# A new table of order and engines for an attention and MLP kernel on one core

## The chip, the cores and the metric
The kernel runs on one NeuronCore of one Trainium2 chip. The core has a matrix engine (TensorE, PE in the profile; PEld is its weight load), a vector engine (VectorE, DVE), an activation engine (ScalarE, ACT), a general engine (GpSimd, POOL) and a queue for DMA issues (SyncE, SP). Each engine carries out its instructions in the order in which they were written for it. The metric is the time of one execution on the device in microseconds (us). Before the change the median of three runs is 287.29 us (285.19 to 288.51).

## The reference
Two layers, one after the other. A linear attention with cosine-weighted features over 8 batches of 576 tokens and 8 heads of 64, and then an MLP without a bias over all 4608 tokens:
```python
def _attn_ref(q, k, v):                 # each 8, 8, 576, 64
    theta = np.pi / 2.0 * pos / S
    def phi(x, c, s):
        r = np.maximum(x, 0.0)
        return np.concatenate([r * c, r * s], axis=-1)
    q_p = phi(q, cos_w, sin_w)
    k_p = phi(k, cos_w, sin_w)
    kv = np.einsum('bhsf,bhsd->bhfd', k_p, v)
    z = np.sum(k_p, axis=2)
    num = np.einsum('bhsf,bhfd->bhsd', q_p, kv)
    den = np.einsum('bhsf,bhf->bhs', q_p, z)[..., None] + 1e-06
    return (num / den).astype(np.float32)

def _moe_ref(x, w_in, w_out):           # 4608x512, 512x2048, 2048x512
    h = x @ w_in
    g = h * np.cos(h)
    return (g @ w_out).astype(np.float32)
```
Inputs and outputs are float32; the kernel multiplies in float16 and sums in float32.

## The kernel before, in words
**Tiling.** The tokens are worked on in nine chunks of 512. Chunk c below 8 is 512 tokens of batch c; the 64 that are left over in each batch make up chunk 8. For each batch there is a load of k, q and v, five token tiles of features (relu times cosine or sine, `prep`, L452 on ScalarE and L453 on VectorE), casts of V to float16 (`cast_v`, L466 ScalarE, L467 VectorE, L468 GpSimd), the product `kv` (L479), and for each token tile the transposed q (`q_pe` on TensorE with its copy at L514 or L516, or `q_dma`, a transposing DMA), the product `num` (L542), the denominator (`den`, L560 or L562), the quotient x (L566, L568), and x transposed (`x_pe`, L588 with its copy at L593, or `x_dma`). Batches 0 and 1 transpose q on TensorE, batches 0, 1 and 2 transpose x there; the others go through DMAs. "First attention" and "second attention" are those of batches 0 and 1.

**The MLP.** `layer1` makes h by chunks of w_in's columns, `gate` takes the cosine on ScalarE (L609, a sine with a shift) and multiplies on VectorE (L614). Chunks 0 and 1 do it plainly (L637), chunk 2 with 512 columns at a time (`layer1_plain`, L677). From chunk 3 on part or all of layer1 is done with seven half-size products in place of eight (`layer1_fast`, L780), which needs sums of the blocks of x (`layer1_sums`, XS, L738) and of w_in (`w_in_sums`, WS, L717). The second layer of chunk 0 is plain (`layer2_plain`: products L880, first copies L889, later sums L892); that of chunk 1 on uses seven products (`layer2`, L948), with sums of blocks of g (S and in place, L926 and L979) and of w_out (T, L904). Its copies out of PSUM stand at L959 and L967, its additions out of PSUM at L963, the very last ones at L1002. `seed` (L663) copies one product's bank to another so that a second product can add to it.

**What sets the order.** Every piece of work is added to a `Plan` as a step, with an engine, an estimated cost, a due time, what it reads and what it writes. Some steps name several engines (`either`: features, V casts, denominators and one PSUM copy, L967). The table `KEYS`, one number for each of the 1407 steps, is a priority. `Plan.forward` (L183) goes through the steps as a list scheduler: it keeps a clock for each engine and a model of the two DMA rings, and takes at each point the ready step with the smallest key among those that can start soon (`PATIENCE`); a step of several engines goes to the one that would finish it first. Then all steps are written out in the order of the start times so found. All of it happens while the program is built; on the chip each engine has a fixed list.

**Loads.** q, k and v of batch 0 are issued on SP first. The weights go through GpSimd's queue: `weights` (L1025) writes one small hold that waits for k (L1027), then issues the four quarters of w_in (L1033, cast from float32 to float16 on the way), then `hold2` (L1037), which waits for the first quarter to land, then two quarters of w_out (L1047). The loads of batch 1 wait for small GpSimd copies into the raw tiles (`hold_raw`, L1052), which read a column of w_in that the quarter named by `GATE1` writes: the third. The last two quarters of w_out follow q of batch 1 (`part_of_w_out`, L1059). By the built program GpSimd issues the quarters of w_in in the order first, third, second, fourth.

**Order around the change.** On TensorE before: layer1 of chunk 0 from 21.45 us, two products of `layer2_plain` from 36.49, the q transpositions of batch 1 (L509), its kv (L479), its num, and the other `layer2_plain` products between. Batch 2's last x transposition is followed directly by the first L677 of chunk 2.

The lines of `Plan` that write out the order, and the copies whose engine was fixed:
```python
        start, done = self.forward([k / 100 for k in KEYS])
        ...
        return sorted(st, key=lambda s: (s["start"], s["n"]))
...
        if eng == "ACT":
            act(0.5, due, lambda: nc.scalar.activation(out=dst, in_=ps, func=AF.Copy), [key], [dkey])
        else:
            dve(0.4, due, lambda: nc.vector.tensor_copy(out=dst, in_=ps), [key], [dkey])
```

Of the kernel before, what the change touches and what calls it, by code (L numbers as in the profile page):

```python
# [125 lines left out]
class Plan:  # L126
# [56 lines left out]
    def forward(self, key):  # L183
# [32 lines left out]
        for n, k in enumerate(left):  # L216
            if not k:
                ask(n)
# [980 lines left out]
```

## Time and profile before
| what | value |
|---|---|
| runs of the kernel before | 285.19, 287.29, 288.51 us |
| the profiled execution | 284.34 us, of which the span from the first to the last instruction is 282.3 us |
| TensorE's mean granted clock | 0.993 |
| busy: PE / PEld / DVE / ACT / POOL | 270.5 / 219.1 / 249.2 / 218.0 / 19.2 us |
| the chain that ended last, by engine | PE 85%, DVE 5%, DMA 4%, ACT 3%, issue 1% |
| bytes moved | 53.30 MB in 77599 packets, a mean of 189 GB/s |
| costliest groups | L609 ScalarE 53.3 us, L614 VectorE 56.7, L948 TensorE 55.9, L452 ScalarE 37.2 and 32.3 |

A group's line reads: line, engine, operation, out<-in (partitions x elements, type), count, busy time, mean duration of one, and the idle time ahead of it with its releaser. Successive instructions of one engine overlap at their ends, so that ScalarE's 128x512 copies, 597 ns long, follow each other every 0.50 us, VectorE's 128x512 operations out of PSUM, 685 ns long, every 0.60 us, and its features, 480 ns long, every 0.40 us. A ScalarE feature of 128x512 takes 715 to 721 ns and follows at 0.61 us. A GpSimd cast of 128x1024 takes 1088 ns, the same cast on VectorE 689 ns. ScalarE takes 1024 ns for the 128x1024 copy of qT, VectorE 687 ns.

### The profile page before, as it was taken

How to read it: one execution, taken by the hardware profiler on the slowest of the kernel's cores; microseconds unless marked ns; L12 is line 12 of the kernel's file. 1: busy time of each engine (PE TensorE's matmuls, PEld its weight loads, DVE VectorE, ACT ScalarE, POOL GpSimd, SP SyncE). 2: the span in 40 equal slices, each digit the busy share in tenths (PEclk: the TensorE clock that was granted, in tenths of full speed). 3: DMA queues.
4: the chain of work that ended last, by engine and by line, in shares of the span. 5: the costliest groups of instructions: out<-in, count | busy, mean ns of one | idle time of the engine just before them, and what ended most of it. 6: DMA issues, size and time to landing. Idle time of an engine off the chain costs nothing.

```text
span 282.3 us, 6870 instructions
## 1 busy us (share of the span) xinstructions
PE 270.5 (96%) x2715; PEld 219.1 (78%) x2715; DVE 249.2 (88%) x443; ACT 218.0 (77%) x396; POOL 19.2 (7%) x32
## 2 busy tenths in 40 slices
PE   7799988999989999999999999999999999999994
PEld 2668956678967667779787988898788888888883
DVE  2877796999999989998999999999999999997952
ACT  2856698896899998599899999996676675877420
POOL 1440020010000010003003000210000000000000
PEclk9799999999999999999999999999999999999999
DMA  6999999969979999997999899988013100300124
GB/s 204 312 200 222 298 291 267 320 133 285 311 231 235 211 229 293 241 310 161 308 234 268 167 275 270 240 117 251 3 37 116 57 2 0 151 0 2 74 77 149
DMA packets 77599, 53.30 MB, mean 189 GB/s; under 512 B 46080, under 2 KB 75264, under 8 KB 77568
## 3 DMA queue, kind: packets, MB, share of 16 engines
q1 hardware_dynamic: 72608, 48.12, 66.7%
q0 software_dynamic: 4224, 4.19, 9.5%
q10 hardware_dynamic: 736, 0.57, 0.6%
q8 instruction: 21, 0.34, 0.5%
q14 instruction: 10, 0.08, 0.1%
HBM read 36.74 MB, written 9.44 MB: 164 GB/s over the span
## 4 chain that ended last, share of the span: by engine, by line
PE 85%; DVE 5%; DMA 4%; ACT 3%; issue 1%; DVEq 0%
PE M L948 32%; PE M L780 15%; PE M L637 10%; PE M L677 7%; PE TR L780 6%; PE M L880 5%; PE ATT L542 3%; DMA xT<-x 2%; PE ATT L479 2%; DMA qm<-in_q_dram 2%; PE M L509 2%; PE ATT L1022 1%; PE TR L677 1%; DVE x L568 1%; ACT xT L593 1%; ACT KQ L452 1%
## 5 line engine op out<-in xcount | busy, mean ns | idle before, releaser
L609 ACT ACTIVATE ch<-M 128x512 f32<-128x512 f32 x90 | 53.3, 597 | 14.4 <-PE M L637 6.9
L614 DVE TENSOR_TENSOR gT<-M,ch 128x512 f16<-128x512 f32 x84 | 56.7, 685 | 5.0 <-ACT ch L609 4.6
L948 PEld LDWEIGHTS <-gT 128*128 128x128 f16 x560 | 54.0, 98 | 7.6 <-DVE gT L926 0.5
L948 PE MATMUL M<-w_out_sb,gT 128*128 128x256 f16 x448 | 55.9, 273 | 0.0
L452 ACT ACTIVATE KQ<-km,CS 128x512 f16<-128x512 f32 x55 | 37.2, 715 | 0.2 <-DMA km<-in_k_dram 0.2
L452 ACT ACTIVATE KQ<-qm,CS 128x512 f16<-128x512 f32 x47 | 32.3, 721 | 4.5 <-DMA qm<-in_q_dram 4.5
L780 PEld LDWEIGHTS <-w_in_sb 128*128 128x128 f16 x320 | 30.8, 98 | 4.3 <-issue 0.2
L948 PE MATMUL M<-T,S 128*128 128x256 f16 x256 | 32.4, 273 | 0.0
L637 PE MATMUL M<-xT,w_in_sb 128*128 128x256 f16 x256 | 30.2, 273 | 0.1
L677 PE MATMUL M<-xT,w_in_sb 128*128 128x512 f16 x112 | 27.6, 379 | 0.8 <-ACT xT L593 0.8
L948 PEld LDWEIGHTS <-S 128*128 128x128 f16 x256 | 24.7, 98 | 4.0 <-issue 0.2
L637 PEld LDWEIGHTS <-w_in_sb 128*128 128x128 f16 x256 | 24.5, 98 | 3.5 <-issue 0.4
L568 DVE TENSOR_TENSOR x<-ATT,rec 128x512 f16<-128x512 f32 x32 | 22.1, 692 | 2.3
L959 ACT ACTIVATE ost<-M 128x512 f32<-128x512 f32 x24 | 14.1, 593 | 12.1 <-PE M L948 9.3
L780 PEld LDWEIGHTS <-WS 128*128 128x128 f16 x216 | 20.5, 98 | 3.3 <-issue 0.5
L677 PEld LDWEIGHTS <-w_in_sb 128*128 128x128 f16 x128 | 12.2, 98 | 10.8 <-issue 0.9
L453 DVE TENSOR_SCALAR KQ<-qm,CS 128x512 f16<-128x512 f32 x33 | 15.4, 498 | 5.1 <-DMA qm<-in_q_dram 5.1
L468 POOL CAST V<-vm 128x1024 f16<-128x1024 f32 (+1 forms) x11 | 10.7, 1004 | 134.9 <-PE M L948 46.0
L542 PEld LDWEIGHTS <-qT 128*128 128x128 f16 x320 | 15.3, 98 | 4.6 <-issue 1.8
L926 DVE TENSOR_TENSOR S<-gT 128x2048 f16<-128x2048 f16 (+1 forms) x16 | 17.4, 1085 | 0.2
L808 DVE TENSOR_TENSOR gT<-Z,ch 128x1024 f16<-128x1024 f32 x13 | 15.9, 1221 | 0.7 <-ACT ch L802 0.4
L542 PE MATMUL ATT<-kvz,qT 128*128 128x65 f16 x288 | 15.7, 194 | 0.6 <-DVE x L568 0.5
(135 smaller groups left out, 461.3 us busy)
## 6 DMA issues: line engine op xcount, KB each, us to landing
out_dram<-ost SPq DMA_DIRECT2D x33, 256.0 KB, 3.0
qm<-in_q_dram SPq DMA_DIRECT2D x8, 640.0 KB, 5.9
km<-in_k_dram SPq DMA_DIRECT2D x8, 640.0 KB, 5.6
qm<-in_q_dram SPq DMA_DIRECT2D x8, 512.0 KB, 6.2
km<-in_k_dram SPq DMA_DIRECT2D x8, 512.0 KB, 5.7
vm<-in_v_dram SPq DMA_DIRECT2D x6, 640.0 KB, 7.2
vm<-in_v_dram SPq DMA_DIRECT2D x6, 512.0 KB, 6.5
w_in_sb<-in_moe_w_in_dram POOLq DMA_DIRECT2D x4, 512.0 KB, 8.9
```

The lines of the kernel that those rows point to most:

```text
L452: fn = {"ACT": lambda: nc.scalar.activation(out=out_, in_=in_, func=AF.Relu, scale=sc), "DVE": lambda: nc.vector.tensor_scalar(out=out_, i ...
L453: "DVE": lambda: nc.vector.tensor_scalar(out=out_, in0=in_, scalar1=0.0, scalar2=sc, op0=ALU.max, op1=ALU.mult)}
L542: nc.tensor.matmul(bank[hb][:, hh * D1:(hh + 1) * D1], lhsT=a[:, h, :], rhs=z[:, h, :], start=(i == 0), stop=(i == len(parts) - 1))
L568: nc.vector.tensor_tensor(out=split(x16[n][:, hs, :], k), in0=A[:, :, :, 0:D], in1=split(rec[n][:, hs], k).unsqueeze(3).broadcast_to((P, k ...
L609: act(0.5, due, lambda: nc.scalar.activation(out=ch[c], in_=bank, func=AF.Sin, bias=math.pi / 2.0, scale=1.0), [key], [("ch", c)])
L614: dve(0.61, due, lambda: nc.vector.tensor_tensor(out=dst, in0=a, in1=b, op=ALU.mult), [key, ("ch", c), *rd], dkeys)
L637: nc.tensor.matmul(M1[m][:, jj * 2 * P:(jj + 1) * 2 * P], lhsT=w_in_sb[:, cc, j * P:(j + 1) * P], rhs=X[:, cc, ts], start=(cc == 0), stop= ...
L677: nc.tensor.matmul(M, lhsT=w_in_sb[:, cc, j * P:(j + 1) * P], rhs=X[:, cc, :], start=(cc == 0), stop=(cc == NCT - 1))
L780: nc.tensor.matmul(bank[0][:, j * TH:(j + 1) * TH], lhsT=a(cc, j), rhs=b[:, cc, :], start=(first and j == 0 and cc == 0), stop=(last and j ...
L808: dve(1.14, due, lambda: nc.vector.tensor_tensor(out=g4, in0=four(uz), in1=four(cc2), op=ALU.mult), zk + ck, [("g", gi(c), h * JH + j, t) ...
L926: dve(0.07 + 1.07 / NG, due, lambda: nc.vector.tensor_tensor(out=out_[:, sl], in0=a[:, sl], in1=b[:, sl], op=op), rd, wr, port=True)
L948: nc.tensor.matmul(bank[0][:, tt * MH:(tt + 1) * MH], lhsT=a[:, j, tt * P:(tt + 1) * P], rhs=b[:, j, :], start=(first and (apart or tt == ...
```

## The change
`KEYS` is no longer a priority but the order itself: each number is a place times ten plus a digit, which names the engine for a step that has several. The scheduler (`forward`, `link` and their constants) is gone; `run` takes the engine and sorts by place. Copies out of PSUM that were fixed to an engine (q transposes, x transposes, `seed`, the copies of `layer1_fast`, `layer2_plain` and `layer2`, and kv's whole copy) go through a helper, `copies`, and can be on either; the sums go through `sums`, which knows only VectorE. `GATE1` names the first quarter of w_in in place of the third. The costs given in `cast_v`, `kv` and others only describe steps and do not enter the program.

By the built programs: the 1407 steps are the same, TensorE's 440 among them in another order. VectorE has 407 steps (402 before), ScalarE 390 (398), GpSimd 29 (26), SP 141 (141). From ScalarE to VectorE go 3 copies of `layer2_plain`, 5 of `x_pe`, 3 of `layer2` and one each of `seed` and `layer1_fast`; the copies of `q_pe` go two each way; 22 features go to VectorE and 26 to ScalarE. GpSimd has 14 casts of V (11 before). The quarters of w_in are issued in the order second, first, fourth, third. On TensorE three `layer2_plain` products stand ahead of the q transpositions of batch 1 and a fourth ahead of its kv; half a `layer2` product stands between batch 2's last x transposition and the first L677.

```diff
 KEYS = (
-    5824, 5995, 5824, 2967, 2673, 126, 143, -359, -2881, 263, -1072, -2121, 539, -49, 2962,
...
+    0, 1060, 530, 0, 0, 710, 1360, 2010, 2660, 3310, 3960, 4610, 9400, 10800, 9900, 12600,
...
     def run(self):
         st = self.steps
         assert len(KEYS) == len(st)
-        start, done = self.forward([k / 100 for k in KEYS])
-        for s, a, b in zip(st, start, done):
-            s["start"], s["end"] = a, b
-        return sorted(st, key=lambda s: (s["start"], s["n"]))
...
+        for s, k in zip(st, KEYS):
+            self.pick(s, k % 10)
+            s["at"] = k // 10
+        assert all(st[d]["at"] < s["at"] for s in st for d in s["deps"])
+        return sorted(st, key=lambda s: (s["at"], s["n"]))
+
+    def pick(self, s, i):
+        if i:
+            e = list(s["opts"])[i - 1]
+            s["opts"] = {e: s["opts"][e]}
             s.update(zip(("eng", "occ", "lat", "fn"), s["opts"][e]))
...
-    GATE1 = (w_in_sb[0:2, 0, Dff // 2 + 1:Dff // 2 + 2], [("w_in", 2)])
+    GATE1 = (w_in_sb[0:2, 0, 1:2], [("w_in", 0)])
...
+    def copies(due, cost, out_, in_, rd, wr, hint):
+        either(due, cost, {
+            "ACT": lambda: nc.scalar.activation(out=out_, in_=in_, func=AF.Copy),
+            "DVE": lambda: nc.vector.tensor_copy(out=out_, in_=in_)}, rd, wr, hint, port=False)
+
+    def sums(due, n, out_, in0, in1, op, rd, wr, lazy=None, rate=0.523e-3):
+        def go(q):
+            return lambda: q.tensor_tensor(out=out_, in0=in0, in1=in1, op=op)
+        either(due, {"DVE": 0.07 + n * rate, }, {"DVE": go(nc.vector)}, rd, wr,
+               lazy=lazy)
...
-        if eng == "ACT":
-            act(0.5, due, lambda: nc.scalar.activation(out=dst, in_=ps, func=AF.Copy), [key], [dkey])
-        else:
-            dve(0.4, due, lambda: nc.vector.tensor_copy(out=dst, in_=ps), [key], [dkey])
+        copies(due, {"ACT": 0.5, "DVE": 0.4}, dst, ps, [key], [dkey], 1 if eng == "ACT" else 2)
...
-        act(0.5, due, lambda: nc.scalar.activation(out=dst[0], in_=bank[0], func=AF.Copy),
-            [bank[1]], [dst[1]])
+        copies(due, {"ACT": 0.5, "DVE": 0.61}, dst[0], bank[0], [bank[1]], [dst[1]], 1)
...
         def copy(dst, bank, dk, due):
-            act(0.5, due, lambda: nc.scalar.activation(out=dst, in_=view(bank), func=AF.Copy),
-                [bank[1]], dk)
+            copies(due, {"ACT": 0.5, "DVE": 0.61}, dst, view(bank), [bank[1]], dk, 1)
```

More of the change, by code (lines that the diff above doesn't have):

```diff
@@ L17 @@
 KEYS = (
[105 rows of a table removed]
[121 rows of a table added]
 )
 class Plan:
-    LINK = {"PE": 0.12, "ACT": 0.05, "DVE": 0.05, "POOL": 0.1, "SP": 0.0}
-    SHARE, WAKE, LAND = {"HW": 0.40, "SW": 0.56}, {"HW": 1.1, "SW": 1.3}, 1.0
-    BUSY = 2.2
-    PATIENCE = {"PE": 0.1, "ACT": 0.25, "DVE": 0.25, "SP": 0.2}
     def __init__(self):
@@ L408, in act, with either @@
         pl.add("ACT", occ, occ + lat, due, fn, rd, wr)
[L410 removed]
+    def either(due, cost, fn, rd, wr, hint=0, port=True, lazy=None):
         lat = {"DVE": 0.13, "ACT": 0.15, "POOL": 0.15}
[L413 removed]
+        pl.add([(e, cost[e], cost[e] + lat[e], fn[e]) for e in cost], 0, 0, due, None, rd, wr,
+               port=port, lazy=lazy, hint=hint)
+    def copies(due, cost, out_, in_, rd, wr, hint):
[7 more added lines that the diff above has]
+               lazy=lazy)
     def tokens(ap):
@@ L464, in cast_v @@
         f = nt * len(heads) / H
-        cost = {"DVE": 0.09 + 0.33 * f, "ACT": 0.12 + 0.5 * f, "POOL": 0.9}
+        cost = {"DVE": 0.07 + 0.33 * f, "ACT": 0.08 + 0.44 * f, "POOL": 0.12 + 0.5 * f}
         fn = {"ACT": lambda: nc.scalar.activation(out=out_, in_=in_, func=AF.Copy),
@@ L496, in kv @@
         else:
-            act(0.6, due, lambda: nc.scalar.activation(
-                out=Z, in_=ATT[:, :, 0:HB * D1], func=AF.Copy), keys, zk)
+            copies(due, {"ACT": 0.5, "DVE": 0.62}, Z, ATT[:, :, 0:HB * D1], keys, zk, 1)
     def qdst(b, t):
@@ L512, in q_pe @@
         pe(H, MMT, due, mm, [("qp", t, g, h) for g in range(2) for h in range(H)] + ["ID"], [key])
-        if eng == "ACT":
-            act(0.95, due, lambda: nc.scalar.activation(out=dst, in_=ps, func=AF.Copy), [key], [dkey])
-        else:
-            dve(0.69, due, lambda: nc.vector.tensor_copy(out=dst, in_=ps), [key], [dkey])
+        copies(due, {"ACT": 0.95, "DVE": 0.69}, dst, ps, [key], [dkey], 1 if eng == "ACT" else 2)
     def q_dma(b, t, due):
@@ L716, in tt @@
             q = [("qT", n // 4)] if g >= OWN and n > 1 else []
-            dve(0.33, due, lambda: nc.vector.tensor_tensor(out=ws[n], in0=a, in1=b, op=op),
-                [("w_in", g // 2), ("w_in", 2 + g // 2)] + rd, wr + [("WS", n, g)] + q, lazy=20.0, port=True)
+            sums(due, CH2 * GW, ws[n], a, b, op, [("w_in", g // 2), ("w_in", 2 + g // 2)] + rd,
+                 wr + [("WS", n, g)] + q, lazy=20.0)
         tt(3, a11, a21, ALU.subtract, [("a21", g)], [])
@@ L737, in tt @@
         def tt(n, a, b, rd, wr=()):
-            dve(0.33, start[c] - 1 + 0.3 * n, lambda: nc.vector.tensor_tensor(
-                out=XS[n], in0=a, in1=b, op=ALU.subtract), xk + rd, [("XS", i, n)] + list(wr), port=True)
+            sums(start[c] - 1 + 0.3 * n, CH2 * TH, XS[n], a, b, ALU.subtract, xk + rd,
+                 [("XS", i, n)] + list(wr))
         tt(0, b12, b11, [], (hk("k") + hk("q") + hk("v") + ["AL"]) if c == B - 1 else
@@ L788, in copy @@
         def copy(dst, bank, key, due):
-            act(0.5, due + 0.3, lambda: nc.scalar.activation(out=dst, in_=bank[0], func=AF.Copy),
-                [bank[1]] + (["AL"] if st_ else []), [key])
+            copies(due + 0.3, {"ACT": 0.5, "DVE": 0.61}, dst, bank[0],
+                   [bank[1]] + (["AL"] if st_ else []), [key], 1)
         def plus(dst, bank, key, due):
@@ L807, in four @@
                 return ap.rearrange("p (h j s) -> p h j s", h=2, j=2)
-            dve(1.14, due, lambda: nc.vector.tensor_tensor(
-                out=g4, in0=four(uz), in1=four(cc2), op=ALU.mult), zk + ck,
-                [("g", gi(c), h * JH + j, t) for h in range(2) for j in (j0, j0 + 1) for t in (2, 3)],
-                port=True)
+            sums(due, 2 * SM, g4, four(uz), four(cc2), ALU.mult, zk + ck,
+                 [("g", gi(c), h * JH + j, t) for h in range(2) for j in (j0, j0 + 1) for t in (2, 3)],
+                 rate=1.045e-3)
         def out(src_, key, hj, ht, due):
@@ L888, in layer2_plain @@
                 if jh == 0:
-                    act(0.5, due + 1.0, lambda O=O, M=M: nc.scalar.activation(
-                        out=O, in_=M, func=AF.Copy), [mk], [ok])
+                    copies(due + 1.0, {"ACT": 0.5, "DVE": 0.61}, O, M, [mk], [ok], 1)
                 else:
@@ L903, in tt @@
         def tt(out_, a, b, op, rd, wr):
-            dve(1.14, start[2] - 8, lambda: nc.vector.tensor_tensor(
-                out=out_, in0=a, in1=b, op=op), rd, wr, port=True)
+            sums(start[2] - 8, JH * MH, out_, a, b, op, rd, wr)
         tt(T3, b22, b12, ALU.subtract, wk, ["T3"])
```

126 lines of the change are left out of this document (6 added, 120 removed), and 224 rows, old and new, of the table KEYS.

## The prediction

> **What bounds the kernel now.** I read the stage table first (busy time of each engine in five stretches of the span), then TensorE's waits, then the chain of waits where TensorE stood still, then GpSimd's timeline where the loads of the weights start.
>
> The stage table, columns PE, PEld, DVE, ACT, POOL (busy us, instructions), granted clock, DMA share, GB/s:
> ```profile
> core 0: us, PE busy (x) PEld busy (x) DVE busy (x) ACT busy (x) POOL busy (x), PEclk, DMA share, GB/s
> 0.00:36.50 36.50, 32.18 (x296) 23.75 (x297) 24.56 (x54) 22.31 (x42) 6.76 (x18) 0.95 1.06 252
> 36.50:53.50 17.00, 15.19 (x184) 9.99 (x183) 13.91 (x37) 15.41 (x30) 1.83 (x3) 1.00 1.11 292
> 53.50:114.00 60.50, 58.94 (x601) 43.76 (x600) 57.26 (x107) 53.81 (x102) 3.11 (x3) 1.00 1.03 244
> 114.00:268.00 154.00, 153.95 (x1545) 132.74 (x1546) 147.77 (x239) 123.71 (x221) 7.54 (x8) 1.00 0.61 148
> ```
> From 114 to 268 us TensorE is busy 153.95 of 154 us: no gain can come from there, only a loss, and VectorE has 154.00 - 147.77 = 6.2 us to spare. What can be won lies before 114 us, where the DMA share is full and TensorE idles 36.50 - 32.18, 17.00 - 15.19 and 60.50 - 58.94 us. The waits say on what (engine and line, what it waited for: us, times, longest):
> ```profile
> PE M L509 <- DVE KQ L453: 2.3, 1, 2.3
> ...
> PE ATT L479 <- DVE V L467: 1.2, 1, 1.2
> PE M L677 <- ACT xT L593: 0.8, 1, 0.8
> PE ATT L542 <- DVE x L568: 0.5, 1, 0.5
> PE M L542 <- DVE kvz L494: 0.5, 1, 0.5
> PE M L780 <- DVE XS L738: 0.3, 1, 0.3
> ```
> The 2.3 us are the first features at the start, which wait for q from memory; the change does not touch that load. The other five, 3.3 us together, stand in three places. First, the attention of batch 1 (chain of waits from 36 to 46 us: start, us, what):
> ```profile
> 36.49 3.45 PE M L880 x16
> 39.94 0.46 PE M L509 x8
> ...
> 41.11 0.41 DVE V L467 x2
> 41.52 0.40 DVE KQ L453
> ...
> 41.98 0.72 ACT V L466 x2
> 42.70 0.61 ACT KQ L452
> 43.31 0.91 ACT qT L514
> 44.22 0.62 ACT KQ L452
> 44.88 0.62 PE M L509 x8
> ```
> TensorE does two products of `layer2_plain`, transposes q, and then needs V (L479), whose casts are not done. Second, at 80.45 us, the xT copy of batch 2. Third, this stretch of the chain from 95 to 116 us:
> ```profile
> 99.36 6.57 DMA xT<-x
> ...
> 106.03 0.74 DVE XS L738
> ...
> 113.18 0.70 DVE x L568
> ```
> GpSimd's timeline shows when loads can start (start, us, line, what, idle before and its releaser):
> ```profile
> 17.64 0.19 POOL L1037 COPY w_out_sb<-w_in_sb 1x4 f16<-1x4 f16 x1 [2.85 <-DMA w_in_sb<-in_moe_w_in_dram]
> 18.14 1.48 POOL L1047 DMA_DIRECT2D w_out_sb<-in_moe_w_out_dram  x2 [0.30 <-POOL w_out_sb L1037]
> 20.29 0.30 POOL L1052 CAST vm<-w_in_sb 2x1 f32<-2x1 f16 x2 [0.68 <-DVE rec L566]
> ```
>
> **The change part by part.** The new table sets the order on every queue and the engine of each copy, feature and cast. The same 1407 steps are issued; TensorE's 440 are the same. By the built program's order, VectorE gains 5 steps net, ScalarE loses 8, GpSimd gains 3.
>
> (1) The order of w_in. The words say first quarter first. In the built order the quarters go 2nd, 1st, 4th, 3rd (before: 1st, 3rd, 2nd, 4th). In before the four land at 17.59, 20.18, 23.08 and 26.04 us, so the first quarter, which layer1 of chunk 0 uses first, comes 2.6 us later, at 20.18. Layer1 starts at 21.45: slack 1.3 us, so nothing is late. I add 0.1 for its start; bounds -0.2 (the cover is loose and the wait for the first quarter is not the last there) and +1.6 (it lands in the third place, 23.08 against 21.45).
>
> (2) GpSimd's queue. The holds of w_out and of batch 1's loads now both wait for the first quarter, so both move from 17.6 to 20.2 us. Behind them one hold, two w_out loads (1.48 us), then the holds for k, q, v: the first load of batch 1 is issued near 20.2 + 0.5 + 0.3 + 1.5 + 0.4 = 22.9 against 20.7. V lands in before at 39.0 to 41.3 us. The 16 DMA engines are full until then (share 1.06 and 1.11), so bytes, not issue times, set the landing: I take +0.5 us, between 0 and 2.3.
>
> (3) Batch 1's attention. Three L880 products now stand ahead of the q transposes and a fourth ahead of L479: 36.49 + 3 x 1.73 + 0.9 + 1.73 = 44.3 us at L479, against 42.97 after the wait in before. After V's last landing (41.27) the new order leaves VectorE two casts, a qT copy behind the transposes (42.6 + 0.69) and two casts of about 0.3, and ScalarE a feature (0.61) and two casts (0.41): V is done between 43.2 and 44.0, and I keep the smaller slack, 0.3. With (2) at +0.5, 0.2 is left of the 1.2, but one of the 0.2 us waits in this stretch goes: -1.2 for both. What is late next is kvz and the x of L568 (0.5 and about 0.6 us), which stay; ScalarE's qT copy for the fifth tile (1.02 us, was VectorE's at 0.69) costs 0.3 and is inside them. Three L889 copies go to VectorE (0.60 each by the pitch of L614's 128x512), which idles 17.00 - 13.91 = 3.1 us there; a feature and an x copy go with them, 0.8, so 2.6 of the 3.1 is spent. Bounds -2.1 (all of the waits of the stretch) and +0.7.
>
> (4) Chunk 2. Between the last x transposition and the first L677 now stands half a layer2 product (L948, 0.87 us): it covers the 0.8 us wait. Take -0.8; bounds -0.9 and 0.
>
> (5) XS and x near 108 and 114 us. The first xT DMA is issued ahead of fewer loads, and the two num of a pair are 3.8 us of TensorE's work apart (1.7 before). Take both waits as gone: -0.8; bounds -1.2 (with the issue gaps behind them) and +0.5 (the DMA no faster, TensorE sooner there).
>
> (6) VectorE and ScalarE from 53.5 to 114. VectorE gives three features net (0.40 each) and two 128x1024 casts (0.69) and takes two x copies (0.40): -1.8. GpSimd takes three casts more. Where a GpSimd cast ran, four VectorE features averaged 648 ns against 480, and one XS sum 745 against 416: 0.17 to 0.33 per cast, +0.5 to +1.0. ScalarE gets about +0.6 against 60.5 - 53.8 = 6.7 idle. No term.
>
> (7) From 114 to 268. Four PSUM copies move to VectorE (4 x 0.60), two features, half a cast and a den leave (0.80 + 0.35 + 0.16): +1.1 against 6.2 spare. GpSimd has as many casts as before. TensorE is full, so I take +0.2; bounds 0 and +1.1 when nothing waits (beyond: a rival). The end: one L959 copy moves to VectorE at 271 us; the last chain (L948, L963, L959, L1002) stays. 0, bounds -0.3 and +0.3.
>
> Sum: +0.1 - 1.2 - 0.8 - 0.8 + 0.2 = **-2.5 us**. The profiled execution took 284.34 us (span 282.3 and 2.0 around it), 3.0 below the median of 287.29 and below all three runs (285.19 to 288.51). The change on the median gives 284.8; on the mean of the four executions, 286.33, it gives 283.8. I take the middle, **284.3**.
>
> A rule against this change: the Trainium skill, "SBUF — State Buffer", section "Who interferes with whom", says VectorE and GpSimd share one port pair under an exclusive lock, and that whoever issues first blocks the other fully. This trace agrees in direction (648 against 480 ns) and not in size; by the rule a cast could stop VectorE for its whole 1.09 us, which is rival D.
>
> **The rivals.**
> A, the DMA gives the gain back: full until 114 us, it lands xT at the same time as before, so TensorE arrives sooner and waits at XS. The 1.2 + 0.8 won before then, less 0.1, and the 0.3 at XS are lost: 284.3 + 2.2 = 286.5. For it: DMA share 1.03, and a 6.57 us transposition on the chain. Against it: x leaves earlier too.
> B, batch 1's loads land late: the whole 2.3 us of (2) pass on, less 0.3 slack, +2.0: 286.3. For it: issue sets the place in the queue. Against: share 1.06 to 1.11.
> C, the other side: VectorE becomes the bound from 114 to 268. The four copies stand in order on VectorE and each waits for a product that has just ended; a whole L948 product is 1.74 us, and behind each stand the gates (L614) and sums (L926) that TensorE needs next. Price: 1.1 + 1.0 (collisions) = 2.1 without any wait, 2.1 + 4 x 1.74 = 9.1 at most. It decides from 2.7 us on (2.5 + 0.2 of the sum), slower than before; the middle of 2.7 and 9.1 is 5.9, 3.2 over break-even: 290.0 on the same middle of footings. For it: 96% busy there and TensorE without slack. Against it: 6.2 us spare, and ScalarE freed of the same copies.
> D, each cast stops VectorE for its whole length: three more casts x 1.09 = 3.3 in 53.5 to 114, less the 1.8 it is relieved of: +1.5 if all of it reaches TensorE, 285.8. For it: 767 ns once; against it: the mean of 648, and 3.2 us idle there.
>
> **How the numbers follow.** About 1% (2.9 us) is what a measurement of this kernel can tell from no change. Forecast 0.45 (its own range 281.3 to 286.0; it lies almost on the 1% line, so 0.28 faster and 0.17 same); A 0.10 (0.01 faster, 0.09 same); B 0.08 (same); C 0.32 (0.10 same, 0.22 slower); D 0.05 (0.01 faster, 0.04 same). Faster 0.30, same 0.48, slower 0.22. The range 281.3 to 290.8: below, the gains at their bounds on the lower footing; above, a little over the middle of C, beyond which some 0.13 is left.
>
> **What would show it.** First L637 near 21.5 us with the first quarter landed near 20.2 (1); first batch-1 load issued near 23 (2); no wait of L479 on V over 0.3 (3); no wait of L677 on xT at 80 (4); no XS wait at 106 to 108 (5); VectorE near 149 busy of 154 and TensorE's idle time there under 0.5 (7). Wrong, if V lands after 42, or if TensorE shows waits on L614, L926 or the moved copies after 114 us.

## The result and the profile after

The changed kernel takes 283.72 us (median of eight runs, 282.68 to 285.48) against 287.25 us (285.12 to 289.04) for the kernel before, measured beside it: a ratio of 0.9892, 95% interval 0.9843 to 0.9941. Measured once more, on the chip of the later experiments, it took 283.66 us (twelve runs) against 285.47 us: 0.9948, interval 0.9918 to 0.9978. The ratios are not quotients of these medians, and those of the experiments leave out 8 of before's 89 runs, which were in a slower state. The gain is real and is 0.5 to 1.1% by the ratios, 1.5 to 3.1 us; by the medians it is 1.8 and 3.5 us. The forecast was 284.3 us.

The two profiled executions differ by less: 284.34 us before, 283.17 us after (span 281.1). Before's profiled execution was quicker than all of its eight timed runs above, but not unusual among the 89 beside the experiments, whose medians are 284.85 to 285.64 us. Lines have moved by the change: in after, L365 and L364 are the features on VectorE and ScalarE, L420 the q transposes, L391 kv, L450 num, L476 x, L514 and L519 the two halves of a gate, L542 layer1 of chunks 0 and 1, L581 `layer1_plain`, L684 `layer1_fast`, L848 `layer2`, L323 every sum, L380 GpSimd's casts of V, L318 and L319 the copies on ScalarE and VectorE. The experiments have the lines of after, since they are made of it.

The stage table of after, columns as before:
```profile
0.00:36.50 36.50, 32.51 (x301) 22.94 (x302) 26.95 (x60) 21.28 (x40) 6.63 (x18) 1.00 1.06 254
36.50:53.50 17.00, 16.23 (x193) 10.53 (x192) 15.74 (x41) 13.63 (x26) 1.67 (x3) 1.00 1.11 295
53.50:114.00 60.50, 58.88 (x613) 44.32 (x611) 57.17 (x103) 54.32 (x103) 6.15 (x6) 1.00 1.06 254
114.00:268.00 154.00, 153.81 (x1534) 131.83 (x1533) 148.19 (x238) 122.95 (x218) 7.37 (x8) 1.00 0.60 143
```
Between 36.5 and 53.5 us TensorE is busy 16.23 us where it was 15.19: that is the attention of batch 1. From 53.5 to 114 us it is no busier than before, though two of its waits were to go there; something took their place. TensorE's waits name it:
```profile
...
PE M L581 <- DVE gT L519: 1.3, 1, 1.3
PE M L420 <- ACT KQ L364: 1.0, 1, 1.0
PE M L391 <- ACT V L378: 0.8, 1, 0.8
PE ATT L450 <- DVE x L476: 0.7, 1, 0.7
PE M L420 <- DVE KQ L365: 0.4, 1, 0.4
PE ATT L450 <- DMA qT<-KQ: 0.3, 1, 0.3
...
```
The waits of L420, and that of L391 on V, belong to the start (batch 0). The wait of kv on V in batch 1 (1.2 us), that of chunk 2's first product on xT (0.8) and that of `layer1_fast` on XS (0.3) are gone. In their place a product of chunk 2 waits 1.3 us for a gate on VectorE. VectorE's timeline shows why the gate is late (start, us, line, what):
```profile
78.66 1.23 DVE L323 TENSOR_TENSOR gT<-gT 128x2048 f16<-128x2048 f16 x1
79.80 1.28 DVE L365 TENSOR_SCALAR KQ<-qm,CS 128x512 f16<-128x512 f32 x1
81.00 0.82 DVE L323 TENSOR_TENSOR WS<-w_in_sb 128x512 f16<-128x512 f16 x1
81.74 1.21 DVE L323 TENSOR_TENSOR T<-w_out_sb,T 128x2048 f16<-128x2048 f16 x1
82.87 1.87 DVE L519 TENSOR_TENSOR gT<-M,ch 128x512 f16<-128x512 f32 x3
```
and GpSimd's for the same time:
```profile
79.17 2.37 POOL L380 CAST V<-vm 128x1024 f16<-128x1024 f32 x2 [20.27 <-DMA vm<-in_v_dram]
```
The feature takes 1.28 us in place of 0.48, the sum 0.82 in place of 0.42, both while GpSimd casts V of batch 3, which VectorE did before. The first of the two casts, a 128x1024, ran from 79.17 to 80.79: 1.62 us, where 1.05 is usual, since it began under VectorE's sum that ran from 78.66 to 79.88. The gate behind them starts at 82.87.

How long TensorE stood still in each kernel is worked out from the starts of successive matmuls in the trace, each start-to-start less the pace of its size in undisturbed rows (0.216 us for 512 columns, 0.109 for 256, 0.057 for a transposition, 0.031 for 65 columns); it counts in the stretch in which it begins. Time that a slower clock takes is in it. One profiled execution each, us:

| kernel | 0-30 | 30-50 | 50-80 | 80-120 | 120-end | sum |
|---|---|---|---|---|---|---|
| before | 7.21 | 2.69 | 0.90 | 1.19 | 0.91 | 12.91 |
| gate1_alone (before's order) | 6.12 | 3.69 | 1.13 | 1.06 | 3.34 | 15.34 |
| after | 6.22 | 1.46 | 0.48 | 1.98 | 1.62 | 11.76 |
| after_again (the same program) | 6.23 | 1.41 | 0.48 | 2.15 | 2.42 | 12.70 |
| early_only | 6.38 | 1.43 | 2.77 | 2.17 | 1.17 | 13.92 |
| late_only | 6.39 | 3.70 | 0.94 | 1.59 | 1.05 | 13.67 |
| gate_first | 6.33 | 1.41 | 0.48 | 1.76 | 1.44 | 11.42 |
| casts_off | 6.12 | 1.42 | 0.47 | 2.30 | 2.75 | 13.06 |
| copies_act | 6.11 | 1.41 | 0.46 | 1.51 | 2.06 | 11.55 |

### The profile page after: what moved, and what is told of

It reads as the page before. It is cut to its first block, busy times and chain, and to the rows that moved or that the text cites. A ratio compares the mean times of both kernels' runs of the same rounds, so it can differ in the third digit from the quotient of the medians.

```text
span 281.1 us, 6887 instructions
## 1 busy us (share of the span) xinstructions
PE 270.5 (96%) x2715; PEld 217.4 (77%) x2715; DVE 253.5 (90%) x448; ACT 214.0 (76%) x388; POOL 21.8 (8%) x35
## 4 chain that ended last, share of the span: by engine, by line
PE 80%; DMA 7%; DVE 7%; ACT 3%; issue 2%; SPq 1%; DVEq 0%; ACTq 0%
PE M L848 30%; PE M L684 14%; PE M L542 10%; PE TR L684 6%; PE M L783 5%; PE M L581 5%; DMA qT<-KQ 4%; PE ATT L450 3%; DMA km<-in_k_dram 3%; PE ATT L391 3%; DVE gT L519 2%; DVE KQ L365 1%; ACT KQ L364 1%; PE TR L581 1%; DVE gT L323 1%
## 5 line engine op out<-in xcount | busy, mean ns | idle before, releaser
L514 ACT ACTIVATE ch<-M 128x512 f32<-128x512 f32 x90 | 52.5, 596 | 12.9 <-PE M L542 5.5
L848 PEld LDWEIGHTS <-gT 128*128 128x128 f16 x560 | 54.0, 98 | 8.8 <-DVE gT L323 0.5
L519 DVE TENSOR_TENSOR gT<-M,ch 128x512 f16<-128x512 f32 x84 | 56.5, 684 | 3.5 <-ACT ch L514 3.1
L848 PE MATMUL M<-w_out_sb,gT 128*128 128x256 f16 x448 | 56.8, 273 | 0.1
L364 ACT ACTIVATE KQ<-km,CS 128x512 f16<-128x512 f32 x55 | 37.8, 722 | 1.3 <-DMA km<-in_k_dram 1.3
L364 ACT ACTIVATE KQ<-qm,CS 128x512 f16<-128x512 f32 x51 | 35.2, 719 | 4.1 <-DMA qm<-in_q_dram 4.1
L684 PEld LDWEIGHTS <-w_in_sb 128*128 128x128 f16 x320 | 30.9, 98 | 4.3 <-issue 0.6
L848 PE MATMUL M<-T,S 128*128 128x256 f16 x256 | 31.7, 273 | 0.0
L318 ACT ACTIVATE ost<-M 128x512 f32<-128x512 f32 x30 | 17.9, 595 | 16.0 <-PE M L848 12.3
L542 PE MATMUL M<-xT,w_in_sb 128*128 128x256 f16 x256 | 29.9, 272 | 0.1
L581 PE MATMUL M<-xT,w_in_sb 128*128 128x512 f16 x112 | 28.1, 379 | 1.3 <-DVE gT L519 1.3
L848 PEld LDWEIGHTS <-S 128*128 128x128 f16 x256 | 24.9, 98 | 4.1
L542 PEld LDWEIGHTS <-w_in_sb 128*128 128x128 f16 x256 | 24.7, 98 | 3.4 <-issue 0.2
L476 DVE TENSOR_TENSOR x<-ATT,rec 128x512 f16<-128x512 f32 x32 | 22.1, 692 | 2.3
L380 POOL CAST V<-vm 128x1024 f16<-128x1024 f32 (+1 forms) x14 | 13.5, 995 | 128.3 <-DMA vm<-in_v_dram 94.2
L684 PEld LDWEIGHTS <-WS 128*128 128x128 f16 x216 | 20.8, 98 | 2.8
L581 PEld LDWEIGHTS <-w_in_sb 128*128 128x128 f16 x128 | 11.7, 98 | 10.5 <-issue 1.5
L365 DVE TENSOR_SCALAR KQ<-qm,CS 128x512 f16<-128x512 f32 x29 | 14.8, 541 | 5.1 <-DMA qm<-in_q_dram 5.1
L450 PEld LDWEIGHTS <-qT 128*128 128x128 f16 x320 | 14.8, 98 | 5.1 <-issue 1.8
L323 DVE TENSOR_TENSOR S<-gT 128x2048 f16<-128x2048 f16 (+1 forms) x16 | 17.4, 1085 | 0.2
L323 DVE TENSOR_TENSOR gT<-Z,ch 128x1024 f16<-128x1024 f32 x13 | 15.9, 1221 | 0.9 <-ACT ch L706 0.8
L450 PE MATMUL ATT<-kvz,qT 128*128 128x65 f16 x288 | 15.0, 194 | 1.3 <-DVE x L476 0.7
```

Source lines behind the costliest of these rows:

```text
L318: "ACT": lambda: nc.scalar.activation(out=out_, in_=in_, func=AF.Copy),
L323: return lambda: q.tensor_tensor(out=out_, in0=in0, in1=in1, op=op)
L364: fn = {"ACT": lambda: nc.scalar.activation(out=out_, in_=in_, func=AF.Relu, scale=sc), "DVE": lambda: nc.vector.tensor_scalar(out=out_, i ...
L365: "DVE": lambda: nc.vector.tensor_scalar(out=out_, in0=in_, scalar1=0.0, scalar2=sc, op0=ALU.max, op1=ALU.mult)}
L450: nc.tensor.matmul(bank[hb][:, hh * D1:(hh + 1) * D1], lhsT=a[:, h, :], rhs=z[:, h, :], start=(i == 0), stop=(i == len(parts) - 1))
L476: nc.vector.tensor_tensor(out=split(x16[n][:, hs, :], k), in0=A[:, :, :, 0:D], in1=split(rec[n][:, hs], k).unsqueeze(3).broadcast_to((P, k ...
```

## The experiments

Every experiment is after with another table `KEYS`. The first edit is shown against before; the others are told in words, against after unless the text says before. gate1_alone, early_only, late_only and feat_to_act ran on one chip, the rest on another; after itself was run beside the second group only.

**The hold alone.** Before's order and engines on every queue, batch 1's loads held by the first quarter.
```diff
-    GATE1 = (w_in_sb[0:2, 0, Dff // 2 + 1:Dff // 2 + 2], [("w_in", 2)])
+    GATE1 = (w_in_sb[0:2, 0, 1:2], [("w_in", 0)])
```


> The order and the engines of the kernel before, on every queue; only the loads of batch 1 wait for the first quarter of w_in in place of the third (the quarters themselves stay in the order 1st, 3rd, 2nd, 4th). My theory: the loads of batch 1 can be issued some 2 us sooner, but the DMA engines are full there, so V lands within 0.5 us of before's 41.27 and the time is that of before within 1 us (ratio 0.997 to 1.003). Rival: the hold was what kept V late, then the wait of L479 on V (1.2 us) shrinks and the ratio is 0.994 to 0.997. A second question: the profiled execution of before, 284.34 us, lies under all eight of its timed runs (285.12 to 289.04). If that execution was an odd one, this kernel's profile shows more waiting on TensorE between 75 and 120 us than the 0.91 + 0.47 + 0.69 us of before.


Measured: 285.59 against 284.85 us, 1.002 (0.9987 to 1.0053): by the time the hold is worth nothing. The loads are issued at 18.93 us in place of 20.74, and V lands 1.0 us sooner (40.26 against 41.27), more than the theory allowed. TensorE comes to kv 1.1 us sooner as well, since it lost 1.1 us less at the start, and so the wait on V is the 1.2 us that it was. The second question is answered with no: from 50 to 120 us this execution stands still for 2.2 us, before's profile for 2.1. It took 286.63 us, though, the longest of its twelve, and shows what a long execution of before's order has more:
```profile
PE ATT L450 <- DMA qT<-KQ: 1.5, 1, 1.5
...
PE ATT L391 <- DVE V L379: 1.2, 1, 1.2
PE M L581 <- ACT xT L318: 0.8, 1, 0.8
PE M L684 <- DVE gT L519: 0.7, 1, 0.7
```
A q transposition by DMA, issued at 160.76, lands at 168.78 us, in before's profile at 166.54, and num waits 1.5 us for it. A gate at 184 us costs 0.7; ahead of it stand two features that took 2.04 us on VectorE, about 0.88 when nothing holds them, while GpSimd casts V:
```profile
181.14 2.99 POOL L380 CAST V<-vm 128x1024 f16<-128x1024 f32 x3 [25.18 <-DMA vm<-in_v_dram]
181.18 2.04 DVE L365 TENSOR_SCALAR KQ<-qm,CS 128x512 f16<-128x512 f32 x2
```
So before's order has collisions of this kind too. Against before's profile the extra standing still is after 120 us, 2.4 us of it, and 1.0 us between 42 and 46 us. The latter is no wait at all, by the granted clock (the column after the busy times):
```profile
36.00:40.00 4.00, 3.84 (x30) 2.14 (x28) 3.60 (x9) 4.00 (x8) 1.48 (x2) 1.00 1.13 313
40.00:42.00 2.00, 0.73 (x10) 0.58 (x9) 2.00 (x9) 2.00 (x6) 0.00 (x0) 1.00 1.23 202
42.00:44.00 2.00, 1.82 (x39) 1.72 (x38) 0.63 (x3) 1.75 (x3) 0.00 (x0) 0.67 1.19 192
44.00:46.00 2.00, 2.00 (x32) 2.00 (x30) 0.69 (x1) 1.71 (x4) 0.00 (x0) 0.50 0.97 275
46.00:50.00 4.00, 4.00 (x45) 2.58 (x44) 3.29 (x13) 2.89 (x7) 0.00 (x0) 0.99 1.08 365
```
After the wait on V the clock is at half for 3.4 us. In before's own profile it stays at 1.00 there:
```profile
42.00:46.00 4.00, 2.66 (x65) 2.36 (x64) 2.17 (x7) 4.00 (x9) 0.00 (x0) 1.00 1.17 193
```

**One part alone.** The steps up to `layer2_plain` of chunk 0 by after's table and the rest by before's, and the other way round.
```diff
 early_only, steps 0 to 251 / steps 252 to 1406
-after's places and engines / after's places and engines
+after's places and engines / before's places and engines
 late_only
-after's places and engines / after's places and engines
+before's places and engines / after's places and engines
```


> After's order and engines for the steps of the first attention, layer1 of chunk 0, batch 1's attention and layer2_plain of chunk 0 (the steps up to about 53 us); before's order and engines for everything later. My theory from the two profiles: TensorE's waiting before 55 us is 1.0 less at the start and 1.2 less in batch 1's attention, so this is 2.2 us faster than before, ratio 0.990 to 0.995, and it keeps before's waits at 80, 108 and 114 us. Rival: the DMA gives it back, TensorE arrives 2 us sooner at chunk 2 and 3 and waits there that much longer, ratio 0.998 to 1.002.

> Before's order and engines for the steps up to the end of layer2_plain of chunk 0, after's for everything later. By the two profiled executions the late part loses 1.1 us (waits on xT, XS and x 1.1 us less, the new wait at 83.6 us 1.5 more, 114 to 268 us 0.7 more): ratio 1.002 to 1.005. By the medians (283.72 against 287.25, 3.5 us, of which 2.2 lie before 55 us) the late part wins 1.3 us: ratio 0.993 to 0.997. The run tells which of the two comparisons is the typical one.


Measured: early_only 285.66 us, 1.0027 (0.9986 to 1.0069); late_only 285.10 us, 1.0014 (0.9986 to 1.0043), both against 284.85. By the intervals neither part gains more than 0.14% by itself. The early part does what was expected up to 50 us (30 to 50 us: 1.43 in place of 2.69 to 3.70 of waiting) and loses 1.9 us of it at the seam between the two orders, where the chain of waits reads:
```profile
56.52 0.89 PE M L542 x8
57.41 0.02 issue
57.43 0.61 ACT ch L514
58.04 0.02 issue
58.06 0.69 DVE gT L519
```
`layer1` of chunk 1 stands still until 58.8 us for a gate whose own product has only just ended: TensorE has used up the work that the old order kept for this place. late_only keeps the 3.7 us in batch 1 and has after's new wait at the gate, 1.47 us. Its second reading (it wins 1.3 us) misses; its first (1.002 to 1.005) lies partly inside the interval. The medians say that the parts do not add, and the seam is a cause that the trace shows; but after was not run on this chip, where the nearest kernel to it, feat_to_act below, gained 0.2% (0.9952 to 1.0005), so the time alone does not show it.

My 2.2 us for the early part was 1.0 us too high already, since the 1.0 us at the start was not the order. In before's profile q landed at 7.52 us (7.01 in gate1_alone, 7.13 in after), and behind the longer wait for it TensorE's clock was at half from 8.5 to 11.9 us, 0.79 on the mean of this stretch (columns as in the stage table):
```profile
8.00:16.00 8.00, 7.40 (x68) 5.43 (x69) 7.20 (x19) 6.50 (x12) 3.60 (x5) 0.79 1.08 277
```
That cost it 1.5 us from 8.6 to 12 us, where the other profiles lose 0.5 or less; none of them has a half clock there, and all stand still for 5.9 to 6.5 us up to 30 us, in either order.

**TensorE's order around batch 1, without the order of the features.**
```diff
 batch 1, TensorE
-2 x layer2_plain, q transposes, kv, ...
+3 x layer2_plain, q transposes, layer2_plain, kv, ...
 layer2_plain's copies
-ScalarE
+VectorE (three of four)
```


> Before's order and engines, except around the attention of batch 1: TensorE's order there is after's (three products of layer2_plain ahead of the q transpositions, one ahead of kv), and the steps of layer2_plain, its copies on VectorE among them, stand as in after. The order of the loads and features of batch 1 stays. My theory: the products cover the wait on V; the waits from 40 to 46 us fall from 2.5 to 0.9 or less and the kernel is 1 to 1.6 us faster than before (ratio 0.994 to 0.997). Rival: the three copies put on VectorE delay its V casts and x, and TensorE waits for x (L476) 1 us more; ratio 0.998 to 1.002.


Measured: 288.91 us, 1.0127 (1.0092 to 1.0163), slower. The wait on V is indeed gone, but the transposes now wait for features that come in another order (1.0 us at 45.6), num for x (0.9) and the x transposes for a qT copy on VectorE (1.4 at 49.6); and then this:
```profile
46.00:50.00 4.00, 2.00 (x44) 1.78 (x42) 3.23 (x11) 1.21 (x3) 0.00 (x0) 1.00 0.99 298
50.00:52.00 2.00, 2.00 (x17) 0.88 (x15) 1.38 (x5) 1.15 (x3) 0.00 (x0) 0.57 1.07 379
52.00:54.00 2.00, 2.00 (x16) 0.88 (x15) 1.42 (x3) 0.00 (x0) 0.00 (x0) 0.58 1.10 357
```
TensorE was busy 2.00 of 4 us, and the next 4 us run at 0.57 and 0.58 of the clock, 4 x 0.42 = 1.7 us lost. Neither the theory nor the rival holds: TensorE's order is worth nothing here without the order of the engines that feed it. Which of the two parts of the edit costs more, TensorE's order or the copies on VectorE, was not separated. The late q transposition (1.8 us at 171.7) and the late gate (0.8 at 187.2) of gate1_alone are in this profile too.

**The collision with GpSimd.** First the features that collide were moved away:
```diff
 VectorE, 79 us and 151 us
-L365 feature (three)
 ScalarE, the same places or just behind
+L364 feature (three)
```


> After, with three q features moved from VectorE to ScalarE: those that stood on VectorE while GpSimd cast V (at 79.80, 151.28 and 151.86 us, lasting 1.28, 0.66 and 1.27 us where 0.48 is usual). My theory: a VectorE feature that starts during a GpSimd cast stands still until the cast ends, and the gates behind it are late, which makes TensorE's wait of 1.47 us before L581 at 83.6 and its 0.54 us at 154; with them gone both fall under 0.4 together and the kernel is 1.2 to 1.8 us faster than after (ratio to before 0.983 to 0.986 if after is 0.989). Rival: the gates are late because VectorE has two sums (0.82 and 1.21 us) ahead of them; then 0.6 us or more of the 1.47 is left and ScalarE's extra 0.6 us shows as a wait on its gates; ratio that of after.


Measured: 284.29 us against 284.85, 0.9979 (0.9952 to 1.0005). The wait at 83 us is still 1.14 us, so the expectation fails. VectorE shows that the theory does not:
```profile
78.45 1.22 DVE L323 TENSOR_TENSOR gT<-gT 128x2048 f16<-128x2048 f16 x1
79.60 1.27 DVE L323 TENSOR_TENSOR WS<-w_in_sb 128x512 f16<-128x512 f16 x1
80.79 1.62 DVE L323 TENSOR_TENSOR T<-w_out_sb,T 128x2048 f16<-128x2048 f16 x1
82.34 1.87 DVE L519 TENSOR_TENSOR gT<-M,ch 128x512 f16<-128x512 f32 x3
```
With the feature gone the next in line, the sum of w_in, stands still in its place (1.27 us, usually 0.42), and the one behind it too (1.62, usually 1.22). ScalarE pays in addition (0.6 us at 156 us). The next three kernels are after once more, after without the cast, and after with VectorE's order turned round.

> The changed kernel itself once more, on the same chip and against the same runs of before as the next three. The first comparison gave a ratio of 0.989 (0.984 to 0.994), while the two profiled executions differ by 1.2 us only (0.996). If the typical gain is that of the profiled pair, the ratio is 0.994 to 0.998 here; if it is that of the medians, 0.987 to 0.991. TensorE's waits should stand again at 47 (0.9 us) and 83.6 (1.5 us), and none over 0.6 us after 100 us.


Measured: 283.66 us against 285.47, 0.9948 (0.9918 to 0.9978); the profile has 0.27 us at 82.4 where after's had 1.47 at 83.6. It is the same program. The cast, which waits for V, started at 80.78 us in place of 79.17:
```profile
80.78 2.41 POOL L380 CAST V<-vm 128x1024 f16<-128x1024 f32 x2 [21.85 <-DMA vm<-in_v_dram]
```
by which time VectorE was through with the feature and the sum of w_in, and had begun the sum of w_out:
```profile
79.77 0.48 DVE L365 TENSOR_SCALAR KQ<-qm,CS 128x512 f16<-128x512 f32 x1
80.16 0.42 DVE L323 TENSOR_TENSOR WS<-w_in_sb 128x512 f16<-128x512 f16 x1
80.50 1.22 DVE L323 TENSOR_TENSOR T<-w_out_sb,T 128x2048 f16<-128x2048 f16 x1
81.64 1.88 DVE L519 TENSOR_TENSOR gT<-M,ch 128x512 f16<-128x512 f32 x3
```
Here it was the cast that stood: its first piece, 128x1024, took 1.85 us, where 1.05 is usual. The collision is worth 1.47 - 0.27 = 1.2 us of TensorE's waiting, and whether it happens hangs on when a load lands (V at 79.03 us in after, 80.63 here). The ratio is the one that I gave for the profiled pair (0.994 to 0.998); that of the first medians (0.987 to 0.991) lies outside the interval. My second point, no wait over 0.6 us after 100 us, was wrong: num waits 1.05 us at 104.6 for the first q transposition of batch 4, which lands at 104.56 us, 5.5 us after its issue (after: 103.18). (The waits view puts this wait down to ScalarE's cosine, which ended within 0.04 us of the landing; in feat_to_act num again starts 0.05 us after the landing, at 104.55.)

```diff
 GpSimd, batch 3
-L380 cast of V (two)
 ScalarE, behind the copy at 85 us
+L378 cast of V (two)
```


> After, with the two V casts of batch 3 that run on GpSimd at 79 to 81.6 us done on ScalarE from about 86 us on. VectorE's order is that of after, so all that goes is what GpSimd does to VectorE there. My theory: a VectorE instruction with a cast, or with two inputs from SBUF, that starts while GpSimd casts stands until the cast is over: the feature at 79.8 (1.28 us) falls to 0.48, the sum at 81.0 (0.82) to 0.42, the gate comes 1.2 us sooner and the wait of 1.47 us falls to 0.2 to 0.5; ScalarE pays 1.6 us which may show as a wait of up to 0.6 on its gates near 87 us. Rival: the wait hangs on the two sums ahead of the gate, not on the casts; then 1.1 us or more of it is left.


Measured: 284.03 us, 0.9961 (0.9935 to 0.9988). The feature takes 0.48 us and the sum 0.42, the wait at the gate is 0.27: the first theory holds. The price is higher than the 0.6 us that I set, because kv of batch 3 needs these casts at 84 us: it waits 1.6 and 0.4 us for them. The time is not better than after's.
```profile
...
PE ATT L391 <- ACT V L378: 1.7, 2, 1.5
...
```

```diff
 VectorE, 80 us
 L365 feature
+L519 gate, L519 gate
 L323 sum of w_in
 L323 sum of w_out
-L519 gate, L519 gate
```


> After, with one change on VectorE: the two gates that TensorE waits for at 83.6 us stand ahead of a sum of w_in blocks (0.82 us) and a sum of w_out blocks (1.21 us) in place of behind them. My theory: the wait of 1.47 us before L581 is VectorE's order and its collisions, and the gate's inputs are ready at 81.2; so the wait falls to 0.3 or less and the kernel is 1.0 to 1.4 us faster than after. Rival: the sums are then late themselves, and TensorE waits 1 us or more at the first product that uses the w_in sums or T4 (before 105 us); time that of after.


Measured: 283.63 us, 0.9943 (0.9916 to 0.9970). The feature collides (1.28 us) and still the wait at 83 us is gone; 0.6 us of it is back at 86.6, where the third gate now stands behind the sums. So 1.47 us became 0.61 by the profile, and the medians do not tell the two apart, 283.63 and 283.66.

**The smaller parts.**
```diff
 GpSimd, order of w_in's quarters
-2nd, 1st, 4th, 3rd
+1st, 2nd, 4th, 3rd
```


> After, with the first quarter of w_in really loaded first: the quarters go 1st, 2nd, 4th, 3rd in place of 2nd, 1st, 4th, 3rd. The holds for w_out and for batch 1's loads come 2.6 us sooner by it. My theory: the first product of layer1 starts at 20.7 us on x, not on w_in (which lands near 19.7 in after), and V of batch 1 lands by the bytes, not by the time of issue; so the time is that of after within 0.6 us (ratio to before 0.993 to 0.997). Rival: the loads behind the holds gain those 2.6 us, V lands 1 us or more sooner than 41.27 and the wait at 47 us shrinks; 0.6 to 1.2 us faster than after.


Measured: 283.87 against 285.64 us, 0.9937 (0.9908 to 0.9966). The first load of batch 1 is issued at 19.23 us (after 22.12), V lands at 40.79 (41.27), TensorE's waiting from 30 to 50 us is 1.41, as in after: nothing. The order of the quarters does not matter here.

```diff
 five PSUM copies after 114 us
-VectorE (L319)
+ScalarE (L318)
```


> After, with the five PSUM copies of the later stages (three of layer2, one seed, one of layer1_fast) back on ScalarE, at the same places. My theory: four of them lie between 114 and 268 us, where VectorE has 6 us to spare and ScalarE 31, so neither is the bound: TensorE's waiting there changes by less than 0.4 us from after's 0.9 to 1.8, ratio that of after. Rival: VectorE's fullness makes the waits at 125 to 128 and 154 us; then these fall below 0.3 together and the kernel is 0.8 us or more faster than after.


Measured: 283.09 us, 0.9901 (0.9866 to 0.9937), the lowest median of all. Its profile still has a wait of 0.5 us for a gate at 153.4 us and 0.9 us for a q transposition at 103.8. Against w_first, measured beside the same runs of before, it is 0.8 us less, within what the intervals leave open: the copies on VectorE bring nothing and may cost half a microsecond. If rival C is at work there, it is worth that and not six.

```diff
 TensorE, chunk 2
 last x transposition of batch 2
-half a layer2 product (L848)
 3 x L581
+half a layer2 product (L848)
```


> After, with one move on TensorE: the half product of layer2 that stands between batch 2's last x transposition and chunk 2's first product stands behind the first three products of chunk 2, as nothing stands there in before. My theory: the wait on the xT copy (0.9 us in before, at 80.45) is back at about 77 to 78 us, 0.6 to 0.9 us, but part of it is won back where the gates of chunk 2 are waited for at 83 us; ratio 0.3 to 0.8 us worse than after. Rival: the wait of before was on ScalarE's queue ahead of the copy and not on the place of the product; then less than 0.3 us shows.


Measured: 284.21 us, 0.9941 (0.9916 to 0.9966), that of after within the intervals. The wait on xT is back:
```profile
...
PE M L848 <- ACT ost L318: 0.7, 1, 0.7
...
PE M L581 <- ACT xT L318: 0.7, 1, 0.7
...
```
0.85 us at 78.0 by the starts, so the half product does cover it. At its new place another wait appears, 0.9 us at 82.4 for ScalarE's copy of the bank that the next product writes. From 50 to 120 us TensorE stands still for 3.3 us, in the two profiles of after for 2.5 and 2.6. By the profiles the half product is worth 0.7 to 0.8 us, which these medians (284.21, and 283.66 in another comparison) cannot settle.

The version that the runs pointed to: gate_first, two gates at 153 us ahead of two features that collide, and a q transposition ahead of loads.
```diff
 SP
+q transposition of batch 3, fifth tile
 three loads of batch 4
-q transposition of batch 3, fifth tile
 VectorE, 152 us
-L365 feature, L365 feature
 L519 gate, L519 gate
+L365 feature, L365 feature
```


> After, with what the runs so far point to: on VectorE the gates that TensorE waits for at 83.6 us ahead of two sums, and two gates at 153 us ahead of two features that stand still under GpSimd's casts; on SP the fifth q transposition of batch 3, whose landing TensorE waits for at 98 to 99 us, ahead of three of the four loads that it stands behind. My theory: waits of 0.3 to 1.5 us at 83, 0.3 to 0.5 at 98 and 0.5 at 154 us fall to 0.6 in sum, 1.0 to 1.5 us faster than after (ratio to before 0.989 to 0.992). Rival: the waits only move, as in the earlier runs with one of them removed, and batch 4's loads, now later, are waited for at 101 to 105 us; time that of after.


Measured: 284.62 us, 0.9959 (0.9931 to 0.9988): not better than after. The rival held. The wait for that transposition is gone, and q of batch 4, now issued behind it, lands at 96.9 us with two features and a gate standing behind it on VectorE:
```profile
89.22 7.73 DMA qm<-in_q_dram
96.94 0.03 issue
96.97 0.88 DVE KQ L365 x2
97.85 0.61 DVE gT L519
```
TensorE waits 1.28 us for the gate. The DMA engines are full there (share 1.18 from 80 to 106 us), and moving this transfer ahead only chose which one is late.

## Why the prediction was right, and where it was not

The time, 283.72 us, and the sum (-2.5 us against 1.5 and 3.1) came out as forecast, in part by luck: the terms did not all do so, and what the sum is measured against was not in it. Between the two profiles that I compared, standing still falls by 1.15 us (12.91 to 11.76), and 1.0 of that lies before 30 us, where the order has no part; by this pair the new order gains next to nothing. Against gate1_alone, before's order in a long execution, it falls by 3.6 us: 2.2 in batch 1, 0.65 in chunk 2 and 1.7 after 120 us, with 0.9 lost from 80 to 120. The measured gain lies between the two.

(1) The start, +0.1: right. The waits to 30 us are 5.9 to 6.5 us in both orders, but 7.2 in the profile that I read. Its stage table showed the half clock (0.95 up to 36.5 us), and the prediction did not read it.

(2) and (3) Batch 1, -1.2: right, and the largest term. The waits from 30 to 50 us fall from 2.69 to between 1.4 and 1.5 in every kernel with after's early part. What is late next is x at 47.2 us, 0.9 by the starts; the prediction named x, at 0.6. V landed at 41.27 us, not 0.5 later. Unforeseen: in two of the three profiles with before's order there (gate1_alone, late_only) the clock drops after the wait on V, and the same term is -2.2 (3.69 to 1.46). The mean granted clock of every run is on record, and one below 0.9955 takes at least one such stretch at half: 31 of the 81 runs of before in the ratios of the experiments have it, and 1 of after's 20 (12 of 94 with its seven variants, 5 of these in feat_to_act). Before's runs with it are 1.1 to 1.4 us longer than its others. I estimate from these numbers that (31/81 - 1/20) x 1.2 = 0.4 us of the mean gain is clock. No run isolates the rest of this term in the time: early_only has it and gains nothing.

(4) Chunk 2, -0.8: half. The waits from 50 to 80 us fall by 0.4 to 0.65; no_half, without it, is not told apart from after by the time.

(5) XS and x near 108 and 114, -0.8: both waits are gone in every kernel with after's late part. But the transposing DMAs of q come in their stead, 0.3 to 0.5 us at 98 to 99 and up to 1.1 at 104.6. That is rival A in small.

(6) VectorE and GpSimd from 53.5 to 114, "no term": this is the step that failed. I priced a collision at 0.17 to 0.33 us per cast, the mean excess of rows of which some had met only the end of a cast, and let 3.2 us of idle time absorb it. They were also the rows of one execution: in gate1_alone, the same order, features took 1.13 us at 56.3 and 1.29 at 181.2. The feature of after stood for 0.80 us and the sum for 0.40 in one collision, and they stand directly ahead of a gate that TensorE waits for: 1.2 us when it happens, nothing when it does not. Rival D, each cast stops VectorE for its whole length, is the mechanism. Of its 1.5 us of loss 1.2 came as waiting, in one of the two profiles of after. The total time does not show it: the execution with this collision took 283.17 us, the one without it 284.09, and casts_off is no faster than after. The rule of the Trainium skill, "SBUF — State Buffer", section "Who interferes with whom", that the one who issues second is blocked fully, agrees with this: the feature at 79.80 us ended at 81.07, 0.3 us after the first cast's end at 80.79, and without a cast it takes 0.48.

(7) From 114 to 268, +0.2: right by the busy time (153.81 of 154 us, before 153.95). By the starts after 120 us it is too small against before's profile (0.91 us; after 1.62 and 2.42) and too large against gate1_alone's (3.34). Of after's, 0.6 and 0.8 us lie between 140 and 160 us, with single waits of up to 0.5 us on a gate (after_again, 154.7), next to GpSimd's casts (a feature of 1.27 us at 151.86). Before's order has 1.7 to 1.8 us on a q transposition near 170 us in two of its four profiles (gate1_alone, pe_b1, not before and early_only); none of the ten with after's late part has it. Rival C did not come: no wait over 0.8 us there in any profile with after's late part.

What stays open: which part of the change the gain in time comes from. Fewer late q transpositions after 120 us may be a part, by two profiles of four against none of ten, but no edit isolates them.

## What to carry to other kernels

Price a collision by the time left of the other engine's instruction, up to its whole length if it was itself held, and not by the mean over all rows that overlap it; and look at what stands behind the one that is stopped: holds of 0.8 and 0.4 us ahead of a gate that TensorE needed cost TensorE all of it, however idle VectorE was on average. When a new order is better, test whether its parts add: here neither half gave a gain that could be measured, and one lost 1.9 us at the seam. Profile the same program twice before reading differences of 1 us.

## What the runs showed that I had not expected

TensorE's clock falls to half without a wholly idle stretch. In gate1_alone TensorE was busy 3.84 of 4 us and then 0.73 of 2, with single waits of at most 1.36 us, and the granted clock then was 0.67 and 0.50 in the next two 2 us stretches; in before's profile the same waits (1.36 us the longest) left it at 1.00. In pe_b1 two stretches at 0.57 and 0.58 make 4 x 0.425 / 0.5 = 3.4 us at half rate. The clock records give the grid: every whole stretch between two changes, in all fourteen profiles, is a multiple of 3.41 us. The four windows of this length just ahead of a half-rate stretch (before up to 8.48 us, gate1_alone up to 42.68, late_only up to 43.15, pe_b1 up to 50.27) hold 2.12 to 2.34 us of standing still, by the starts; of the other windows at full rate, from 3 us on to the last matmuls, none holds more than 2.14. The waits in before's batch 1 fall into two windows, 1.50 and 1.25 us, and cost no clock. So the edge lies near 2.1 of 3.41 us in these runs. The Trainium skill, "TensorE: Matmul & The Clock Gate", section "Part 1: The HAM clock gate (the "warmup" mystery)", states a free-running window of about 3.4 us and the half rate after an idle window: the length and the dependence on phase agree with these runs, but a window that is partly busy was enough here. So covering the waits of batch 1 took 1.25 us of standing still away and, where the clock had dropped, another microsecond.

In after's profile VectorE also stands still with no cast on GpSimd: two features and two of V's casts between 11 and 15 us, while GpSimd issues w_in's loads, took 0.76 and 0.61 us (0.48 is usual) and 0.48 and 0.52 us (0.28), and a feature at 37.2 us, during the w_out issues, 0.72 us.
